# Attention, a gated MLP and a convolved MLP on one core: the first batch's strided heads divided in time, and its first 288 tokens mixed and multiplied on their own

## The chip, the cores and the metric

The kernel runs on one core of one Trainium2 chip. The metric is the device time of one execution in microseconds (us), the median of three runs. The core's engines are TensorE (PE in the profile; its weight loads are PEld), VectorE (DVE), ScalarE (ACT), GpSimd (POOL) and SyncE (SP), which here issues most of the transfers.

## The reference

Four batches of 576 tokens pass through three layers. The second and third work on 512 channels with 1024 hidden ones.

```python
# attention: 8 heads of 64; rel = query - key
mask_local = (rel >= 0) & (rel < 32)                                  # heads 0 to 3
mask_strided = (rel >= 0) & (pos[None, :] % 32 == pos[:, None] % 32)  # heads 4 to 7
attn = softmax(where(mask, q @ k.T / 8, -1e9))
x = attn @ v                                # (4, 576, 512)
# first MLP: each token is mixed with the one before it
xk = mu_k * x + (1 - mu_k) * x_prev
xr = mu_r * x + (1 - mu_r) * x_prev
x = sigmoid(xr @ w_r) * (relu(xk @ w_k) ** 2 @ w_v)
# second MLP, with a convolution over three tokens
h = relu(x @ w_in)
out = (h * sigmoid(conv3(h, conv_w))) @ w_out
```

The weights arrive as 64-bit floats.

## The kernel before

Channels lie on partitions and tokens on columns. A batch of 576 tokens is two chunks of T = 288 tokens, so chunks 0 and 1 are batch 0. Every product of the MLPs is taken with operands divided into a high and a low part (`hi` and `lo`), as three matmuls: high by high, low by high, high by low. `products` issues them for 128 output channels and 288 tokens, per 128 input channels (L789).

**Attention** goes head pair by head pair: p = 0 and 1 are the local heads, p = 2 and 3 the strided ones, two heads in one pair. `load` fetches the pair's queries and keys (tile `qk`) and values (`vt`); `unit(b, p, half, loaded)` computes one half of a pair: scores into PSUM (L594), mask and row maximum on VectorE (L610), exponentials on ScalarE with the row's sum read behind each (L615), one division of the unit on VectorE (L626), transposes on TensorE (L638, L648), a copy to SBUF on either engine (L396/L398 or L657/L659), values on TensorE (L671, L680) and a copy into `xT` (L716 and others). For a local pair a half is a range of tokens: five blocks of 64 queries, then four. For a strided pair it is a range of residues modulo 32: a block holds 3 residues at all 18 of their positions, 54 queries by 54 keys, six blocks in one half and five in the other. So each half of a strided pair has tokens from the whole batch, and no token of the batch is complete before all eight units are. Batch 0's local units have their own form (`wide`: 96 keys, one transpose a block); its strided ones have the form of the other batches.

**Mixing** (`mix`) makes xr or xk for one chunk, or for both chunks of batch 0 at once. For each of four channel tiles it is a scale on ScalarE (L768), a multiply-add on VectorE (L769), a rounding to the high part on ScalarE (L770) and a subtraction for the low part on VectorE (L771).

**Weights** come in pieces of 128 x 512 double words (`fetch`, two buffers `raw`). `narrow` makes 32-bit floats of one (a scale, L411, on ScalarE or VectorE; two shifts and an OR on VectorE, L418, L419, L422), `bring` rounds and subtracts (L461 on ScalarE, L462 on VectorE). w_r is four pieces, w_k and w_v eight each.

**Order.** All work is entered as jobs in a `Plan`, with what they read and write, their cost on each engine that can do them, and their buffers (`bufs`). A list scheduler (`search`, `run`) places the jobs by time and rank when the program is built, over and over with the disturbances whose seeds stand in `STEPS`, and each engine's instructions are issued in the order found. While TensorE would wait, `stir` puts matmuls on idle data into the order (L956). `BEHIND` names the score jobs behind which the first two weight pieces are fetched, `MIXES` the buffers of `mix`. The jobs of batch 0 are entered so: attention of the whole batch; `mix((0, 1), "r", ...)`; each piece of w_r with its products for chunk 0 and chunk 1 (`group_r`, closed by a tanh on ScalarE, L801); `mix((0, 1), "k", ...)`; attention of batch 1; each piece of w_k with its products (a column f, `group_k`) for chunk 0 and chunk 1. Three PSUM banks (`mm`) hold the sums of these products.

Of the kernel before, what the change touches and what calls it, by code (L numbers as in the profile page):

```python
# [15 lines left out]
P = 128  # L16
# [11 lines left out]
WARM, MIXES, BEHIND = 10, 2, (0, 3)  # L28
# [8 lines left out]
STEPS = ((40300000007, 40300000026, 40300000031, 40300000050, 40300000114, 40300000121, 40300000163, 40300000246, 40300000278, 40300000284,  # L37
# [13 lines left out]
HALF_ARRAY = {"sc", "pv"}  # L51
BLOCKS = ("B11", "B21", "B22", "T4", "T1", "T2", "T3")
# [288 lines left out]
def block_kernel(ctx, tc, qkL, qkS, vL, vW, vS, mu_k, mu_r, w_k, w_v, w_r, w_in, conv_w, w_out, ident, mask_l, mask_w, mask_s, out):  # L341
# [13 lines left out]
    ms_sb = const.tile([P, SQ], F32, name="ms_sb")  # L355
# [159 lines left out]

    xT = {}
    unit_before, first_scores, late = [None], [], []

    def load(b, p):

        ns = sum(SB) * SQ
# [200 lines left out]
    def attention(b):  # L722
        xT[b] = space(wx, f"xT{b}", [P, KT, S + 1], tag="xT", bufs=2, parts=9)
        plan.add({"POOL": 0.1}, lambda e: pool.memset(xT[b]()[:, :, 0:1], 0.0), [], [(xT[b], 8)])
        for p in range(4):
            loaded = load(b, p)
            if b == 0 and p == 0:
                consts()
# [563 lines left out]
```

## Time and profile before

| | us |
|---|---|
| median of 3 runs | 509.87 (509.21 to 509.95) |
| the profiled execution | 508.81 |
| its span, first to last instruction | 507.0 |
| TensorE busy in the span | 498.2 |
| VectorE busy | 426.0 |
| ScalarE busy | 390.0 |

The span is a little shorter than the profiled execution's own time, and that one lies below the median of the runs. A busy engine is not an engine at its peak: idle matmuls count as busy too.

### The profile page before, as it was taken

Reading aid. Unit: us, or ns where it says so; the run is one execution under the profiler, and the core shown is the slowest. Engines: PE = TensorE matmul, PEld = TensorE weight load, DVE = VectorE, ACT = ScalarE, POOL = GpSimd, SP = SyncE. Lnnn points to the kernel's source line nnn. Section 1 sums busy time; section 2 is a strip of 40 time slices with the busy share of each in tenths; the row PEclk is TensorE's granted clock in tenths of the full one; section 3 lists DMA queues with packets and bytes.
Section 4 is the critical chain, followed back from the end, with each engine's and each line's share of the span. In section 5 each row is a group of like instructions: output and inputs, shape, how many; then the busy total and the mean of one; then the engine's idle time right before and its main releaser. Section 6 shows DMA issues by size and latency. Waiting matters only on the chain.

```text
span 507.0 us, 13536 instructions
## 1 busy us (share of the span) xinstructions
PE 498.2 (98%) x5114; PEld 480.6 (95%) x5114; DVE 426.0 (84%) x1198; ACT 390.0 (77%) x1137; POOL 1.6 (0%) x15
## 2 busy tenths in 40 slices
PE   8889999999999999999999999999999999999997
PEld 5679999989999999999999999899999999999997
DVE  4999899989757899877899833689999995999993
ACT  5999997999848999758979564487778676767852
POOL 0000000000000000000000000000000000000000
PEclk9999999999999999999999999999999999999999
DMA  8955656994286784676466799938029117200111
GB/s 282 364 185 176 200 187 191 316 307 151 100 268 223 227 277 150 229 247 204 154 200 223 249 309 397 343 110 315 24 64 312 36 22 273 94 35 14 48 48 70
DMA packets 57921, 96.61 MB, mean 191 GB/s; under 512 B 4864, under 2 KB 41984, under 8 KB 57600
## 3 DMA queue, kind: packets, MB, share of 16 engines
q1 hardware_dynamic: 57568, 95.58, 55.4%
q8 instruction: 40, 0.66, 0.6%
q14 instruction: 25, 0.20, 0.1%
q10 hardware_dynamic: 288, 0.16, 0.1%
HBM read 63.95 MB, written 31.78 MB: 189 GB/s over the span
## 4 chain that ended last, share of the span: by engine, by line
PE 88%; ACT 5%; DMA 4%; DVE 2%; issue 1%; SPq 0%; ACTq 0%
PE mm L789 47%; PE hh L1042 17%; PE oz L1139 10%; PE ov L1139 8%; PE sc L594 3%; DMA x_d<-xo 2%; PE pv L680 2%; PE tr L648 1%; DMA raw<-in_w_in 1%; ACT pr L615 1%; DMA qk<-in_qkL 1%; ACT wb L411 1%; ACT mx L768 1%; DVE pr L610 0%; ACT Y L770 0%
## 5 line engine op out<-in xcount | busy, mean ns | idle before, releaser
L789 PE MATMUL mm<-X,wvh 128*128 128x288 f32 x448 | 84.5, 298 | 0.0
L1042 PE MATMUL hh<-x,wi 128*128 128x288 f32 x504 | 75.0, 297 | 1.1 <-ACT b L1050 0.6
L1042 PEld LDWEIGHTS hh<-x,wi 128*128 128x128 f32 x504 | 69.6, 188 | 2.2 <-ACT a L1050 0.9
L789 PE MATMUL mm<-Y,wkh 128*128 128x288 f32 x384 | 68.2, 295 | 0.2 <-ACT rs L801 0.2
L789 PEld LDWEIGHTS mm<-X,wvh 128*128 128x128 f32 x448 | 67.0, 188 | 0.3
L789 PEld LDWEIGHTS mm<-Y,wkh 128*128 128x128 f32 x384 | 56.4, 188 | 0.5 <-ACT rs L801 0.4
L615 ACT ACTIVATE pr<-pr,nmx 128x54 f32<-128x54 f32 (+2 forms) x160 | 53.5, 342 | 4.4 <-DVE nmx L610 4.4
L789 PE MATMUL mm<-Y,wrh 128*128 128x288 f32 x256 | 55.9, 301 | 0.6 <-DVE Y L771 0.3
L1096 DVE SCALAR_TENSOR_TENSOR graw<-hb,cw_sb,graw 128x576 f32<-128x576 f32 x64 | 51.0, 810 | 1.8 <-ACT graw L1091 1.3
L789 PE MATMUL mm<-X,wvl 128*128 128x288 f32 x224 | 47.9, 295 | 0.0
L1115 DVE TENSOR_TENSOR blk<-graw,blk 128x576 fp32r<-128x576 f32 x56 | 40.8, 751 | 6.3 <-ACT blk L1114 6.1
L1114 ACT ACTIVATE blk<-graw 128x576 fp32r<-128x576 f32 x56 | 36.4, 678 | 11.1 <-DVE graw L1120 5.0
L789 PEld LDWEIGHTS mm<-Y,wrh 128*128 128x128 f32 x256 | 42.1, 188 | 1.9 <-DVE Y L771 0.8
L789 PE MATMUL mm<-Y,wkl 128*128 128x288 f32 x192 | 40.8, 294 | 0.0
L789 PE MATMUL mm<-Y,wrl 128*128 128x288 f32 x128 | 38.0, 297 | 0.3 <-DVE wrl L462 0.3
L830 DVE TENSOR_TENSOR X<-sq,X 128x288 fp32r<-128x288 f32 x48 | 21.6, 456 | 19.3 <-ACT X L828 15.0
L789 PEld LDWEIGHTS mm<-X,wvl 128*128 128x128 f32 x224 | 35.9, 188 | 0.0
L615 ACT ACTIVATION_READ_ACCUMULATOR pr<-pr,nmx 128x1 f32 x160 | 31.5, 197 | 0.0
L812 ACT ACTIVATE rl<-mm 128x288 f32<-128x288 f32 x64 | 25.7, 403 | 6.7 <-PE mm L789 6.5
L789 PEld LDWEIGHTS mm<-Y,wkl 128*128 128x128 f32 x192 | 30.7, 188 | 0.0
L1139 PE MATMUL oz<-blk,wo 128*128 128x288 f32 x192 | 30.1, 296 | 0.0
L1097 ACT ACTIVATE graw<-graw 128x576 f32<-128x576 f32 x32 | 21.8, 681 | 9.8 <-DVE graw L1096 9.7
(165 smaller groups left out, 1238.4 us busy)
## 6 DMA issues: line engine op xcount, KB each, us to landing
x_d<-xo SPq DMA_DIRECT2D x42, 288.0 KB, 3.2
x<-x_d SPq DMA_DIRECT2D x21, 576.0 KB, 4.8
wi_d<-ws SPq DMA_DIRECT2D x24, 256.0 KB, 3.7
wo_d<-ws SPq DMA_DIRECT2D x24, 256.0 KB, 2.9
wi<-wi_d SPq DMA_DIRECT2D x6, 896.0 KB, 9.2
qk<-in_qkS SPq DMA_DIRECT2D x8, 599.0 KB, 5.3
out<-ob SPq DMA_DIRECT2D x32, 144.0 KB, 1.7
qk<-in_qkL SPq DMA_DIRECT2D x7, 592.0 KB, 5.1
```

Source lines behind the costliest of these rows:

```text
L594: pe.matmul(bank_of[j]()[to + u:to + u + m, at_[j]:at_[j] + nk], qk()[r, qo[j] + u:qo[j] + u + m], qk()[r, ko[j] + u:ko[j] + u + nk], star ...
L615: act.activation(pr()[:, k], pr()[:, k], AF.Exp, bias=nmx()[:, i:i + 1], scale=-1.0, accum_out=sums()[:, i:i + 1])
L680: pe.matmul(outs_[odd]()[r, i * nq + u:i * nq + u + m], vt()[part, v, r], pt()[part, o:o + m], start=True, stop=True)
L789: pe.matmul(o(), w_cols(name, j, t, part), x_[t](), start=(t == 0 and part == 0 and x_ is xhi), stop=(t == nk - 1 and x_ is xlo))
L812: plan.add({"ACT": 0.295}, lambda e: act.activation(r(), o(), AF.Relu), [o], [r])
L830: plan.add({"DVE": 0.37}, lambda e: dve.tensor_tensor(l_(), sq(), h_().bitcast(F32), ALU.subtract), [sq, h_], [l_])
L1042: pe.matmul(o(), w(hw, j), x()[:, hx, j], start=anew and n == 0 and j == 0, stop=last and n == 2 and j == 1, skip_group_check=True)
L1096: plan.add({"DVE": 0.735}, lambda e, k=k: dve.scalar_tensor_tensor(c(), h()[:, k:k + S], cw_sb[:, k * NF + f:k * NF + f + 1], c(), ALU.mul ...
L1097: plan.add({"ACT": 0.6}, lambda e: act.activation(c(), c(), AF.Sigmoid), [mine], [mine], table="sigmoid")
L1114: plan.add({"ACT": 0.13 + S / 1400}, lambda e, w=w, x=x: act.activation(w()[:, 0], x(), AF.Copy), [mine], [(w, 0)])
L1115: plan.add({"DVE": 0.07 + S / 960}, lambda e, w=w, x=x: dve.tensor_tensor(w()[:, 1], x(), w()[:, 0].bitcast(F32), ALU.subtract), [mine, (w ...
L1139: pe.matmul(o(), w_[s_][1](hw, q), x_()[:, hx, s_], start=anew and m == 0 and i == 0 and s_ == 0, stop=last and m == 1 and i == 2 and s_ = ...
```

## The change

For batch 0 the two halves of a strided pair become halves of time. A block now holds 7 residues at the 9 positions of one half of the tokens: 63 queries. The first half (tokens 0 to 287) sees 63 keys, the second 126, the keys of both halves. Five blocks cover the 32 residues; the last one overlaps the one before it, and only 4 of its residues are stored. These units take the `wide` form: one transpose a block, two copies, values with one PSUM bank. Queries and keys of batch 0 are laid out and loaded for each half on its own (`load_half`), the local ones too.

`attention` can be entered for one half. The jobs of batch 0 are now entered in this order: the first half of all four pairs; mixing r of chunk 0 and its products; mixing k of chunk 0; the second half of all four pairs; mixing r of chunk 1 and its products; mixing k of chunk 1. The four mixings have 288 columns, with three buffers of that size in place of two of 576. There are three `vt` buffers in place of four, the `pr` tile grows from 480 to 630 columns, the second weight piece is fetched behind another score job, and `STEPS` has other seeds for the first of its two plans.

```diff
-WARM, MIXES, BEHIND = 10, 2, (0, 3)
+WARM, MIXES, BEHIND = 10, 3, (0, 2)
...
+CG, CI, CN, VTS = 7, NI // 2, 5, 3
+CQ = CG * CI
...
+    def load_half(p, half):
+
+        qk = space(at, "qk", [P, 2 * sum(SB) * SQ + LQ - SQ], bufs=3, parts=2)
+        vt = space(at, "vt", [P, 6, P], bufs=VTS)
+        row, from_ = P * 4, ((qk0, qk1) if p < 2 else (qkA, qkB))[half]
+        n = from_.shape[-1]
+        if p == 0 and half == 0:
+            cut = 2 * LQ * LEAD + STRIDE
+            dma(lambda: qk()[:, :cut], lambda: from_[p, :, :cut], row * cut, [], [(qk, 0)])
+            dma(lambda: mw_sb, lambda: mask_w, P * 2 * LW * 4, [], [fixed["mw"]], "ACT")
+            dma(lambda: qk()[:, cut:n], lambda: from_[p, :, cut:], row * (n - cut), [], [(qk, 1)])
+            dma(lambda: id_sb, lambda: ident, row * P, [], [fixed["id"]], "ACT")
+        else:
+            dma(lambda: qk()[:, :n], lambda: from_[p % 2], row * n, [], [qk])
+        if p < 2:
+            dma(lambda: vt()[:LW, :LB[half]], lambda: vW[p, :, LB[0] * half:LB[0] * half + LB[half]], LW * 4 * P * LB[half], [], [vt])
+        else:
+            nk = CQ * (1 + half)
+            dma(lambda: vt()[:nk, :CN], lambda: vC[p - 2, :nk], nk * 4 * P * CN, [], [vt])
+        return qk, [vt, vt]
...
-        wide = local and b == 0
-        nb, nq, nk, rows = (LB[half], LQ, LW if wide else LK, P) if local else (SB[half], SQ, SQ, SR)
+        wide = b == 0
+        nb, nq, nk, rows = (LB[half], LQ, LW if wide else LK, P) if local else (CN, CQ, CQ * (1 + half), P) if wide else (SB[half], SQ, SQ, SR)
...
-        pr = space(at, "pr", [P, LB[0] * LW], bufs=3, parts=2)
+        pr = space(at, "pr", [P, 2 * CQ * CN], bufs=3, parts=2)
...
-        if wide:
+        if wide and not local:
+
+            def place(e):
+                d = x()[:, p, 1:].rearrange("p (i r) -> p i r", r=STRIDE)[:, CI * half:CI * half + CI]
+                v = out_()[:, :n].rearrange("p (n i g) -> p n i g", n=nb, i=CI)
+                m = CG * (nb - 1)
+                for d_, v_ in ((d[:, :, :m].rearrange("p i (n g) -> p n i g", g=CG), v[:, :nb - 1]), (d[:, :, m:], v[:, nb - 1, :, CG * nb - STRIDE:])):
+                    if e == "ACT":
+                        act.activation(d_, v_, AF.Copy)
+                    else:
+                        dve.tensor_copy(d_, v_)
+
+            plan.add({"ACT": 0.17 + n / 1400, "DVE": 0.13 + n / 960}, place, outs_, [(x, 2 * p + half)])
+        elif wide:
...
-            y = space(wa, "mx", [P, S], bufs=MIXES)
+            y = space(wa, "mx", [P, T], bufs=MIXES)
...
-    attention(0)
-
-    mix((0, 1), "r", "Y", 0)
+    attention(0, (0,))
+    mix((0,), "r", "Y", 0)
     for m in range(KT):
         bring("wr", m)
-        for c in range(2):
-            group_r(c, m)
-    mix((0, 1), "k", "X", 0)
+        group_r(0, m)
+    mix((0,), "k", "X", 0)
+    attention(0, (1,))
+    mix((1,), "r", "Y", 1)
+    for m in range(KT):
+        group_r(1, m)
+    mix((1,), "k", "X", 1)
     attention(1)
```

## Rows read from the trace of the kernel before

**Rows 1.** Busy time by stretches: us, busy us (x instructions) of each engine, clock, DMA.

```profile
35.44:43.50 8.06, 8.06 (x60) 8.06 (x61) 8.06 (x20) 8.06 (x20) 0.00 (x0) 1.00 0.46 152
43.50:50.20 6.70, 6.70 (x81) 6.45 (x79) 6.68 (x21) 5.50 (x13) 0.00 (x0) 1.00 0.53 169
```

**Rows 2.** TensorE in order of time: start us, us, what, idle before it.

```profile
26.95 0.53 PE L956 MATMUL pv<-idle 128*128 128x288 bf16 x3
...
28.23 0.40 PE L789 MATMUL mm<-Y,wrh 128*128 128x288 f32 x1
...
35.44 0.40 PE L789 MATMUL mm<-Y,wrh 128*128 128x288 f32 x1 [0.28 <-ACT rs L801]
...
43.51 0.43 PE L789 MATMUL mm<-X,wkh 128*128 128x288 f32 x2
...
45.99 0.45 PE L594 MATMUL sc<-qk 64*32 64x64 f32 x32
```

**Rows 3.** ScalarE in order of time, from 47.9 us.

```profile
47.91 0.45 ACT L817 ACTIVATE sq<-rl 128x288 f32<-128x288 f32 x1
48.27 0.41 ACT L812 ACTIVATE rl<-mm 128x288 f32<-128x288 f32 x1
```

**Rows 4.** Groups by form, 10.46 to 50.2 us: busy us, mean ns of one, idle before.

```profile
L615 ACT ACTIVATE pr<-pr,nmx 128x54 f32<-128x54 f32 x22 | 7.2, 341 | 0.0
L422 DVE SCALAR_TENSOR_TENSOR wt<-wb,wt 128x512 int32<-128x512 int32 x8 | 5.4, 687 | 0.0
L610 DVE CUSTOM_DVE_ANT_0 pr<-sc,ms_sb 128x54 f32<-128x54 f32 x22 | 3.3, 199 | 0.0
L615 ACT ACTIVATE pr<-pr,nmx 128x96 f32<-128x96 f32 x9 | 3.2, 363 | 0.0
L615 ACT ACTIVATE pr<-pr,nmx 128x64 f32<-128x64 f32 x5 | 1.7, 344 | 0.0
L610 DVE CUSTOM_DVE_ANT_0 pr<-sc,ml_sb 128x64 f32<-128x64 f32 x9 | 1.5, 216 | 0.0
L610 DVE CUSTOM_DVE_ANT_0 pr<-sc,mw_sb 128x96 f32<-128x96 f32 x6 | 1.3, 254 | 0.2 <-PE sc L594 0.2
L396 ACT ACTIVATE pt<-tr 96x384 f32<-96x384 f32 x2 | 1.0, 484 | 1.1 <-PE tr L638 1.1
L626 DVE TENSOR_TENSOR pr<-pr,rec 128x324 f32<-128x324 f32 x2 | 1.0, 476 | 0.0
L626 DVE TENSOR_TENSOR pr<-pr,rec 128x480 f32<-128x480 f32 x1 | 0.7, 654 | 0.0
L657 ACT ACTIVATE pt<-tr 118x354 f32<-118x354 f32 x1 | 0.5, 487 | 0.0
L396 ACT ACTIVATE pt<-tr 96x256 f32<-96x256 f32 x1 | 0.4, 366 | 0.0
```

**Rows 5.** The same view: the mixing of 576 columns, for r.

```profile
L769 DVE SCALAR_TENSOR_TENSOR mx<-xT,mur_sb,mx 128x576 f32<-128x576 f32 x4 | 3.2, 808 | 0.0
L768 ACT ACTIVATE mx<-xT,mur_sb 128x576 f32<-128x576 f32 x4 | 3.1, 781 | 0.0
L771 DVE TENSOR_TENSOR Y<-mx,Y 128x576 fp32r<-128x576 f32 x4 | 2.9, 747 | 0.0
L770 ACT ACTIVATE Y<-mx 128x576 fp32r<-128x576 f32 x4 | 2.6, 695 | 0.0
```

**Rows 6.** Groups by form, 95 to 180 us: the mixing of 288 columns.

```profile
L771 DVE TENSOR_TENSOR Y<-mx,Y 128x288 fp32r<-128x288 f32 x18 | 8.0, 453 | 0.2 <-ACT Y L770 0.2
L770 ACT ACTIVATE Y<-mx 128x288 fp32r<-128x288 f32 x18 | 7.8, 443 | 0.0
L768 ACT ACTIVATE mx<-xT,mur_sb 128x288 f32<-128x288 f32 x10 | 5.2, 531 | 0.0
L769 DVE SCALAR_TENSOR_TENSOR mx<-xT,mur_sb,mx 128x288 f32<-128x288 f32 x9 | 4.5, 512 | 0.8 <-ACT mx L768 0.7
```

**Rows 7.** Busy time by stretches again, from 5 to 10 us.

```profile
5.00:10.00 5.00, 4.98 (x52) 3.33 (x53) 3.04 (x24) 3.44 (x18) 0.00 (x0) 1.00 1.03 329
```

More of the change, by code (lines that the diff above doesn't have):

```diff
@@ L340, in block_kernel @@
 @with_exitstack
-def block_kernel(ctx, tc, qkL, qkS, vL, vW, vS, mu_k, mu_r, w_k, w_v, w_r, w_in, conv_w, w_out, ident, mask_l, mask_w, mask_s, out):
+def block_kernel(ctx, tc, qk0, qk1, qkA, qkB, qkL, qkS, vL, vW, vC, vS, mu_k, mu_r, w_k, w_v, w_r, w_in, conv_w, w_out, ident, mask_l, mask_w, mask_s, mask_c, out):
     nc = tc.nc
@@ L355, in block_kernel @@
     ms_sb = const.tile([P, SQ], F32, name="ms_sb")
+    mc_sb = const.tile([P, 2 * CQ], F32, name="mc_sb")
     muk_sb = const.tile([P, KT], F32, name="muk_sb")
@@ L557, in unit @@
             mask = fixed["mw" if wide else "ml"]
-            qo = [LQ * j + (S + STRIDE) * (j >= LEAD) for j in range(first, first + nb)]
-            ko = [LQ * LEAD + LQ * (first + j) for j in range(nb)]
+            n1 = LEAD * LQ if not wide else (LEAD, LB[1])[half] * LQ
+            lead = (S if not wide else LB[0] * LQ) + STRIDE
+            at0 = 0 if wide else first
+            qo = [LQ * j + lead * (not (wide and half) and j >= LEAD) for j in range(at0, at0 + nb)]
+            ko = [n1 + LQ * (at0 + j) for j in range(nb)]
+        elif wide:
+            masks, mask = [mc_sb[:, CQ * (1 - half):]] * nb, fixed["mc"]
+            qo, ko = [CQ * j for j in range(nb)], [CQ * nb + 1 + nk * j for j in range(nb)]
         else:
@@ L720, in unit, with attention @@
             plan.add({"ACT": 0.085 * (2 + half) + n / 1400, "DVE": 0.065 * (2 + half) + n / 960}, place, outs_, [(x, 2 * p + half)])
-    def attention(b):
-        xT[b] = space(wx, f"xT{b}", [P, KT, S + 1], tag="xT", bufs=2, parts=9)
-        plan.add({"POOL": 0.1}, lambda e: pool.memset(xT[b]()[:, :, 0:1], 0.0), [], [(xT[b], 8)])
+    def attention(b, halves=range(2)):
+        if b not in xT:
+            xT[b] = space(wx, f"xT{b}", [P, KT, S + 1], tag="xT", bufs=2, parts=9)
+            plan.add({"POOL": 0.1}, lambda e: pool.memset(xT[b]()[:, :, 0:1], 0.0), [], [(xT[b], 8)])
         for p in range(4):
-            loaded = load(b, p)
-            if b == 0 and p == 0:
-                consts()
-            for half in range(2):
+            if b:
+                loaded = load(b, p)
+            for half in halves:
+                if not b:
+                    loaded = load_half(p, half)
+                    if p == half == 0:
+                        consts()
                 unit(b, p, half, loaded)
     def consts():
-        for name, t, x, nb in (("ml", ml_sb, mask_l, P * 2 * LK * 4), ("ms", ms_sb, mask_s, P * SQ * 4), ("muk", muk_sb, mu_k, 2048), ("mur", mur_sb, mu_r, 2048)):
+        for name, t, x, nb in (("ml", ml_sb, mask_l, P * 2 * LK * 4), ("mc", mc_sb, mask_c, P * 2 * CQ * 4), ("ms", ms_sb, mask_s, P * SQ * 4), ("muk", muk_sb, mu_k, 2048), ("mur", mur_sb, mu_r, 2048)):
             late.append(dma(lambda t=t: t, lambda x=x: x, nb, [], [fixed[name]]))
@@ L1226, in _layout @@
     ql, kl = heads_t(q[:, :h]), heads_t(k[:, :h])
-    qkL = np.concatenate([ql[..., :n0], lead, kl, ql[..., n0:]], axis=-1)
+    qkL = np.concatenate([ql[..., :n0], lead, kl, ql[..., n0:]], axis=-1)[1:]
+    m0 = LQ * LB[0]
+    qk0 = np.concatenate([ql[0, ..., :n0], lead[0], kl[0, ..., :m0], ql[0, ..., n0:m0]], axis=-1)
+    qk1 = np.concatenate([ql[0, ..., m0:], kl[0, ..., m0 - STRIDE:]], axis=-1)
+    part = [np.concatenate([(i * STRIDE + r0 + np.arange(CG)) for i in range(NI)]) for r0 in [*range(0, CG * (CN - 1), CG), STRIDE - CG]]
+    lo, hi_, both = [np.concatenate([x[c] for x in part]) for c in (slice(0, CQ), slice(CQ, None), slice(None))]
+    qs, ks = heads_t(q[:, h:])[0], heads_t(k[:, h:])[0]
+    qkA = np.concatenate([qs[..., lo], lead[0, ..., :1], ks[..., lo]], axis=-1)
+    qkB = np.concatenate([qs[..., hi_], lead[0, ..., :1], ks[..., both]], axis=-1)
+    vC = np.ascontiguousarray(v[0, h:][:, both].reshape(2, 2, CN, 2 * CQ, D).transpose(0, 3, 2, 1, 4)).reshape(2, 2 * CQ, CN, 2 * D)
     qkS = np.concatenate([heads_t(q[:, h:, order]), lead[..., :LQ - SQ], heads_t(k[:, h:, order])], axis=-1)
```

40 lines of the change are left out of this document (17 added, 23 removed), and 17 rows, old and new, of the table STEPS.

## The prediction

> **What bounds the kernel now.** I read first the busy time by stretches, then TensorE in order of time over the first 60 us, then the groups by form for what the vector engines do there. TensorE reaches its first useful product of the MLP at 28.23 us; before that it computes only the small matmuls of attention, and idle matmuls fill its holes [rows 2]. Its last wait of any size in the first half of the program ends at 35.44 us; from there it is busy the whole of each stretch, at a granted clock of 1.00 [rows 1, 2]. So a microsecond is won only if TensorE has done more useful work by the time its work becomes continuous, and is then never short again. What feeds it until then is ScalarE and VectorE: from 35.44 to 43.50 us both are busy for 8.06 of 8.06 us, and VectorE for 6.68 of the 6.70 after that [rows 1]. They are the second bound, and the tighter one while the first weight pieces are prepared.
>
> TensorE's side in numbers. A product of 128x288 lands every 0.1325 us when nothing is in its way: from 35.44 to 43.51 us stand 60 of them in 8.07 us [rows 1, 2]. The r products of batch 0 are 2 x 4 x 12 = 96, so 36 of them are done at 35.44. The k products begin at 43.51; two columns f of both halves are 48 products, 6.4 us, and with the scores at 45.99 in between [rows 2] the third column is due at about 50.2 us.
>
> **The change, part by part.** *Moved:* the 48 r products of tokens 0 to 287 (6.4 us) no longer need the second half of attention. They need four units of softmax instead of eight, four mixed tiles of 288 columns and the four pieces of w_r. Tile by tile the second half follows, and the k mixing of the first half can go ahead of that of the second.
>
> *Added on ScalarE and VectorE, attention.* An instruction starts about 0.1 us before the row of the one ahead of it ends: the square at 47.91 is 0.45 long and the next starts at 48.27 [rows 3]. I count an instruction at its duration less 0.1 on ScalarE and less 0.08 on VectorE. For each of the two strided pairs of batch 0, eleven blocks of 54 become five of 63 and five of 126. No row has these widths; they lie between and just beyond the rows of 54 and 96.
> - Exponentials: 11 x 341 ns against 5 x (346 + 379), on the line through 341 and 363: 3.75 to 3.63, -0.1 us [rows 4]. The read of the sum that follows each costs about the 0.1 that overlaps.
> - Masks: 199 and 254 ns; on their line 211 and 293, less overlap: +0.35 us [rows 4].
> - Normalising: 324 and 270 elements become 315 and 630; 1.14 ns an element from 476 and 654 ns gives +0.4 us [rows 4].
> - Transposed weights to SBUF: one copy of 354 columns a unit (487 ns) becomes 384 and 256 (484 and 366): +0.26 a unit, +0.5 us [rows 4].
> - Placing the result: as many elements, two copies in place of two or three: 0.
>
> That is about 1.15 us for each pair, 2.3 us for both.
>
> The Trainium skill ("ScalarE: Activation LUTs", section "What ACT_TABLE_LOAD costs") gives an activation with a bias pointer 280 ns plus 0.833 ns a column, a steeper line than the two rows give; by it, as an estimate, 332 and 385 ns, and the sum would be 0.1 us lower.
>
> *Added, mixing.* Eight tiles of 576 columns become sixteen of 288. From the rows, two of 288 against one of 576, with one overlap less: the scale 2 x 0.43 - 0.68 = 0.18; the multiply-add 2 x 0.43 - 0.73 = 0.13; the rounding 2 x 0.34 - 0.59 = 0.09; the subtraction 2 x 0.37 - 0.67 = 0.07 [rows 5, 6]. 0.47 us a tile, 3.7 us for eight.
>
> So ScalarE and VectorE together get 6.0 us more work, 3.0 each if the copies balance them.
>
> *Added on TensorE.* Ten transposes instead of six a pair, wider scores and values: I estimate 1.4 us a pair, 2.8 in all, from bounds of zero (all in holes) and 2.8 (none). It falls where TensorE waits or computes idle matmuls, as at 26.95 [rows 2], so I take zero. Without that cover it would cost the 2.8.
>
> *Transfers.* Batch 0's loads grow from 11 to 17 (and one more mask), from 4.0 to 4.6 MB by their shapes; but what the first half needs is 2.1 MB. The transfer engines are full from 5 to 10 us, at 329 GB/s [rows 7], so 0.6 MB is 1.8 us of theirs; what lies behind it on SP's queue is w_r's pieces and batch 1's loads. Batch 1's are not wanted until long after, and w_r's now come ahead of the second half's loads. The third unit's data come earlier: 592 + 592 KB stand ahead of it now, about 1.15 MB with masks and v tiles then, 0.1 us of transfer sooner, or 0.6 if the v tiles are put behind; I take 0.3. Three vt and three qk buffers hold a half each, not two halves, so no load waits longer than now. The larger pr tile and the third mx buffer cost no instruction.
>
> **The sum.** What stands against the 6.0 us is slack before the third k column: up to 50.2 us ScalarE has 1.2 us idle [rows 1]; five exponentials and nine masks of batch 1 are done early, 5 x 0.34 + 9 x 0.15 = 3.0 us [rows 4]; and the fourth piece of w_k is almost through, five instructions bounded by 0.6 each [rows 4], which I take at 2.4. Together 6.6 us of the two engines. The extra work just fits: (6.6 - 6.0)/2 = 0.3 us to spare. The k mixing of the second half of tokens, 4 x 1.57 = 6.3 us of the two engines [rows 6], may also wait, which is worth between 0 and 3.1 us; I take 0.2, near nothing, because the second half's products are what TensorE wants next. With that and 0.3 from the earlier data, the two engines allow the whole train of products to come 0.8 us sooner. TensorE's side would allow more (rival A), so the two engines decide: span 507.0 - 0.8 = 506.2. The profiled execution took 508.8, 1.8 us around its span; the median is 509.9, 1.1 above the profiled one. Forecast: 506.2 + 1.8 + 1.1 = 509.1 us. A difference below 0.2%, 1.0 us, is about what a measurement of this kernel can't tell from none; the forecast lies just inside it. Its own range is a gain of 2 to a loss of 0.5 us: 507.9 to 510.4.
>
> **Rivals.**
> A, the products' lead survives. If the two engines have more to put off than I counted, only TensorE's supply decides. At 35.44 us 36 products are done; in the new order all 48 of the first half could be, and 27 of the second (three banks open, nine products each for tiles 0 to 2): 39 more, 5.2 us. If all of the 3.0 us delays the last mixed tile, 2.2 remain. I take 3.0: 506.9. For it: both engines are busy in [rows 1] also with things not due. Against it: the third column.
> B, slower: the two engines lose time early. From 5 to 10 us they are busy 6.5 of 10 us, because few units are in flight [rows 7]. In the new order four chains must run out before the first mixing is complete, and with the slack gone every idle microsecond of both engines is one of the kernel. TensorE's order is fixed at build time, so a product that waits for a late tile also holds the transposes and values of the second half queued behind it, and the copies that wait for those. The same hole once more, 1.8 us each, gives 509.1 + 1.8 = 510.9. It decides as soon as the idle time of the two engines between 10 and 46 us, now nearly nothing, passes about 1.5 us each.
> C, the order does not change: a job's place comes from ranks and times, not from where it is written. If the first product still starts after 27 us, the extra work meets the slack and nothing is won: 509.9 to 511.
> D, the clock. It is 1.00 in every stretch, in which holes are filled [rows 1]. The new order has a hole between the first half's products and the second's. If the clock fell to 1.2 GHz there, the 48 products of the second half would take twice 6.4 us, of which I count half as felt: 512.3. The Trainium skill ("TensorE: Matmul & The Clock Gate", "HAM oscillation — how this bites in real kernels") tells of bursts that each start cold behind a wait; the trace shows no such thing here.
>
> **Chances.** Forecast 0.42 (of it 0.13 faster by over 0.2%, 0.27 within, 0.02 slower); A 0.27, faster; B 0.21 (0.18 slower, 0.03 within); C 0.08 (0.05 within, 0.03 slower); D 0.02. Faster 0.40, same 0.35, slower 0.25. The range must take in A with an error of 0.7 and B with 0.6: 506.2 to 511.5.
>
> **What would show it.** First product of the MLP before 24 us, 48 of them before the second half's last values: the move is right. Exponentials of 63 and 126 columns near 346 and 379 ns, mixing near 0.47 us more a tile: the prices are right. ScalarE and VectorE without idle time from 10 to 50 us, and little of batch 1's softmax before 50 us: the slack was spent as I say. The third k column at about 49.4 us: the sum is right; well before 48, A. The forecast is wrong if TensorE waits on the vector engines between 30 and 50 us (B), or if its work is continuous with no such wait from an earlier time on (A).

## The result, and the profile after

| kernel | median us | range | runs | ratio to before, 95% interval |
|---|---|---|---|---|
| before (in the same comparison) | 509.55 | 508.56 to 509.95 | 6 | |
| changed | 514.66 | 513.33 to 517.19 | 6 | 1.0108 [1.0084, 1.0133] |
| changed, again, in a later comparison | 516.23 | 514.73 to 519.23 | 6 | 1.0140 [1.0112, 1.0169] |

The change makes the kernel 5.1 us slower (7.2 in the later one); 509.1 was forecast, and 514.7 lies above the range of 506.2 to 511.5. The profiled execution of the changed kernel took 515.11 us with a span of 513.3, 6.3 more than before's 507.0.

Busy time by stretches in the changed kernel (answers to [rows 1, 7]; us, busy us of TensorE, its weight loads, VectorE, ScalarE, GpSimd, then clock, DMA share, GB/s):

```profile
5.00:10.00 5.00, 4.25 (x63) 2.62 (x59) 3.56 (x32) 4.09 (x23) 0.00 (x0) 1.00 1.04 298
25.00:30.00 5.00, 4.50 (x67) 3.69 (x68) 3.34 (x17) 3.60 (x12) 0.00 (x0) 1.00 1.09 258
30.00:35.00 5.00, 2.51 (x32) 2.08 (x30) 4.37 (x11) 4.37 (x15) 0.00 (x0) 1.00 0.82 255
35.44:43.50 8.06, 8.06 (x129) 7.29 (x129) 8.06 (x31) 7.92 (x26) 0.00 (x0) 1.00 0.55 164
43.50:50.20 6.70, 6.70 (x53) 6.70 (x52) 6.70 (x22) 6.70 (x18) 0.00 (x0) 1.00 0.79 249
```

TensorE in order of time, changed kernel (answers to [rows 2]):

```profile
21.82 0.40 PE L825 MATMUL mm<-Y,wrh 128*128 128x288 f32 x1
...
29.45 0.30 PE L825 MATMUL mm<-Y,wrh 128*128 128x288 f32 x1
29.59 1.03 PE L995 MATMUL pv<-idle 128*128 128x288 bf16 x7
33.11 0.69 PE L690 MATMUL pv<-pt,vt 96*64 96x64 f32 x16 [2.49 <-ACT pt L398]
...
46.83 0.43 PE L825 MATMUL mm<-X,wkh 128*128 128x288 f32 x2
...
73.47 0.42 PE L825 MATMUL mm<-Y,wvh 128*128 128x288 f32 x2
```

The first r product comes 6.4 us sooner, at 21.82. But the products stop at 29.6 us with 24 of 96 done; idle matmuls fill one microsecond, then TensorE stands for 2.49. At 35.44 us, where the kernel before has 36 r products behind it, this one has 30. The k products begin at 46.83 instead of 43.51, the V products (those with w_v) at 73.47 instead of 69.55. The lead is gone before the second half's attention is through. Both kernels have done their 288 r and k products by the first V product. Of the 3.9 us up to there, TensorE is idle for 1.7 us more (6.1 for 4.4) and busy for 2.2 us more, about 1.0 of that with idle matmuls (55 for 42).

Waits of the changed kernel, 20 to 50 us (us in total, times, longest):

```profile
PE pv L690 <- ACT pt L398: 2.5, 1, 2.5
DVE wt L420 <- DMA raw<-in_w_r: 2.3, 1, 2.3
ACT wb L413 <- DMA raw<-in_w_r: 2.0, 1, 2.0
```

TensorE waits for a copy of ScalarE, and ScalarE and VectorE, just before, for the fourth piece of w_r. It was issued at 21.95 us behind two loads of batch 1 of 592 KB (15.78 and 19.41) and took 8.7 us. The DMA views from 5 to 30 us and of the w_r pieces from 0 to 35 us show the queue, first changed, then before (packets, MB, share of 16 engines; then KB each and median us to landing):

```profile
DMA packets 5013, 7.46 MB, mean 298 GB/s; under 512 B 882, under 2 KB 3410, under 8 KB 5009
...
q1 hardware_dynamic: 5009, 7.41, 104.0%
...
raw<-in_w_r SPq DMA_DIRECT2D x4, 512.0 KB, 7.8
```

```profile
DMA packets 4203, 7.96 MB, mean 318 GB/s; under 512 B 736, under 2 KB 2400, under 8 KB 4198
...
q1 hardware_dynamic: 4198, 7.89, 92.0%
...
raw<-in_w_r SPq DMA_DIRECT2D x4, 512.0 KB, 4.7
```

In these 25 us the transfer engines are busier (104% for 92%) and bring less (7.46 MB for 7.96), in more and smaller packets (1.49 KB for 1.89 on average). In the kernel before they have little left to do from 25 us on; in the changed one they are still full there (1.09):

```profile
25.00:30.00 5.00, 4.30 (x66) 3.23 (x64) 4.99 (x17) 5.00 (x16) 0.00 (x0) 1.00 0.59 192
```

In the whole program the changed kernel reads 64.61 MB for 63.95.

Groups by form, 10.46 to 50.2 us, changed kernel (answers to [rows 4 to 6]; busy us, mean ns of one, idle before):

```profile
L634 ACT ACTIVATE pr<-pr,nmx 128x126 f32<-128x126 f32 x10 | 3.9, 400 | 0.0
...
L634 ACT ACTIVATE pr<-pr,nmx 128x63 f32<-128x63 f32 x8 | 2.6, 332 | 0.0
...
L629 DVE CUSTOM_DVE_ANT_0 pr<-sc,mc_sb 128x126 f32<-128x126 f32 x10 | 2.3, 274 | 0.0
...
L645 DVE TENSOR_TENSOR pr<-pr,rec 128x630 f32<-128x630 f32 x2 | 1.6, 808 | 0.0
...
L645 DVE TENSOR_TENSOR pr<-pr,rec 128x315 f32<-128x315 f32 x2 | 1.0, 482 | 0.0
...
L629 DVE CUSTOM_DVE_ANT_0 pr<-sc,mc_sb 128x63 f32<-128x63 f32 x5 | 0.9, 218 | 0.0
...
L398 ACT ACTIVATE pt<-tr 126x256 f32<-126x256 f32 x2 | 0.8, 406 | 0.0
```

Exponentials of 332 and 400 ns (346 and 379 foreseen), masks of 218 and 274 (211 and 293), normalising of 482 and 808; the r mixing of 288 columns takes 562, 506, 475 and 444 ns where [rows 6] has 531, 512, 443 and 453. On the engines whose rows priced them, the single instructions were right within 40 ns; the widest misses are a copy of 256 columns (406 for 366) and the scale and the rounding of the mixing (31 and 32 ns each). The Trainium skill ("ScalarE: Activation LUTs", "What ACT_TABLE_LOAD costs") gave 332 and 385 ns by its line; the first agrees, the second is 15 ns short of the measured 400, so the two measured points lie on a steeper line than the page's.

### The profile page after: what moved, and what is told of

The parts are those of the page before. It is cut to its first block, busy times and chain, and to the rows that moved or that the text cites. A ratio compares the mean times of both kernels' runs of the same rounds, so it can differ in the third digit from the quotient of the medians.

```text
span 513.3 us, 13583 instructions
## 1 busy us (share of the span) xinstructions
PE 501.3 (98%) x5119; PEld 482.9 (94%) x5119; DVE 430.2 (84%) x1215; ACT 389.2 (76%) x1144; POOL 1.7 (0%) x15
## 3 DMA queue, kind: packets, MB, share of 16 engines
HBM read 64.61 MB, written 31.78 MB: 188 GB/s over the span
## 4 chain that ended last, share of the span: by engine, by line
PE 78%; DMA 9%; ACT 7%; DVE 4%; issue 1%; ACTq 0%; SPq 0%
PE mm L825 39%; PE hh L1081 16%; PE oz L1178 10%; PE ov L1178 8%; DMA x_d<-xo 2%; ACT pr L634 2%; DMA raw<-in_w_r 2%; PE sc L613 1%; DMA raw<-in_w_v 1%; DMA wi_d<-ws 1%; PE pv L699 1%; DMA raw<-in_w_in 1%; ACT mx L804 1%; PE tr L667 1%; PE pv L690 1%
## 5 line engine op out<-in xcount | busy, mean ns | idle before, releaser
L1081 PEld LDWEIGHTS hh<-x,wi 128*128 128x128 f32 x504 | 69.5, 188 | 2.2 <-ACT a L1089 0.9
L825 PE MATMUL mm<-Y,wrh 128*128 128x288 f32 x256 | 57.8, 303 | 0.6 <-ACT rs L837 0.4
L634 ACT ACTIVATE pr<-pr,nmx 128x54 f32<-128x54 f32 (+4 forms) x158 | 53.7, 351 | 3.1 <-DVE nmx L629 3.0
L825 PE MATMUL mm<-X,wvl 128*128 128x288 f32 x224 | 47.9, 295 | 0.0
```

Of the source, the lines that this page charges most:

```text
L634: act.activation(pr()[:, k], pr()[:, k], AF.Exp, bias=nmx()[:, i:i + 1], scale=-1.0, accum_out=sums()[:, i:i + 1])
L825: pe.matmul(o(), w_cols(name, j, t, part), x_[t](), start=(t == 0 and part == 0 and x_ is xhi), stop=(t == nk - 1 and x_ is xlo))
L1081: pe.matmul(o(), w(hw, j), x()[:, hx, j], start=anew and n == 0 and j == 0, stop=last and n == 2 and j == 1, skip_group_check=True)
```

## The experiments

Two theories stood at first. *Late load:* the changed kernel loses what the vector engines wait for a load. *Engine work:* it loses what 6 us of additional ScalarE and VectorE work take. Others came with the runs: TensorE full from 33 us on; the transfers as a whole; the order. Where an expectation speaks of theory 1 and theory 2, it means engine work and TensorE. Times are medians of all runs of a version; each profile is of one execution only.

| version | ratio to before, 95% interval |
|---|---|
| early_wr | 1.0100 [1.0064, 1.0136] |
| late_b1 | 1.0131 [1.0080, 1.0183] |
| aligned | 1.0109 [1.0072, 1.0146] |
| before_more_work | 1.0072 [1.0049, 1.0094] |
| before_mix_halves | 1.0040 [1.0016, 1.0065] |
| before_less_pe | 0.9996 [0.9976, 1.0017] |
| after_less_pe | 1.0086 [1.0056, 1.0115] |
| after_less_mix | 1.0128 [1.0096, 1.0159] |
| mask_early | 1.0145 [1.0121, 1.0169] |
| mask_early_wr | 1.0116 [1.0087, 1.0145] |
| mask_early_wr_less_mix | 1.0080 [1.0061, 1.0098] |
| after_light_loads | 1.0093 [1.0073, 1.0112] |
| before_more_loads | 1.0045 [1.0028, 1.0062] |
| after_replanned | 1.0282 [1.0255, 1.0308] |
| before_replanned | 1.0050 [1.0033, 1.0067] |
| after_replanned_first | 1.0200 [1.0177, 1.0223] |
| before_replanned_first | 0.9981 [0.9965, 0.9997] |

Those whose names begin with "before" are edits of the kernel before, the others of the changed one.

### One load at a time

The fourth w_r piece gets a buffer that is free until later, and is issued right behind the third (early_wr):

```diff
-        raw = space(stg, "raw", [P, WC, 2], I32, bufs=2)
+        raw = space(stg, "raw", [P, WC, 2], I32, bufs=2) if fetched[0] != 3 else <a view of an unused "rs" tile>
+            order: job 125 (fourth w_r piece) right behind job 114 (third)
```

> The changed kernel with every engine's order as it is, but the fourth piece of w_r gets a buffer of its own and is fetched right behind the third, ahead of batch 1's queries and keys. Theory (late piece): both vector engines stand still from 28.2 to 30.6 us because this piece lands at 30.6; with the piece in place the wait of 2.0 and 2.3 us is gone, TensorE's wait of 2.5 us at 30.6 too, and the kernel is 1.8 to 2.6 us faster than the changed kernel (ratio to the kernel before 1.005 to 1.007 in place of 1.011). Rival (engine work alone: the 6 us more work of ScalarE and VectorE sets the time, the wait only uses time that is lost anyway): less than 0.7 us faster, ratio 1.0095 or more.

515.08 us, ratio 1.0100: no gain that can be told. Busy time by stretches:

```profile
10.00:15.00 5.00, 3.07 (x43) 2.16 (x44) 3.58 (x29) 3.47 (x20) 0.00 (x0) 0.76 0.90 292
15.00:20.00 5.00, 4.71 (x80) 3.58 (x78) 3.72 (x18) 3.99 (x16) 0.00 (x0) 0.89 0.97 300
...
25.00:30.00 5.00, 4.26 (x43) 3.08 (x42) 5.00 (x20) 5.00 (x20) 0.00 (x0) 1.00 1.04 227
30.00:35.00 5.00, 4.67 (x82) 3.85 (x81) 5.00 (x18) 5.00 (x16) 0.00 (x0) 1.00 1.05 295
```

The wait at 25 to 35 us is gone: both engines are busy throughout. But time is lost before: from 10 to 20 us VectorE works 7.3 us where the changed kernel's first profile has 9.32, and the clock falls below 1. VectorE waited 2.1 us there for the new mask of the strided heads, which had landed 7.0 us after its issue (4.8 us in the first profile). Whether the move caused that is asked below.

The opposite move holds back batch 1's first two q/k loads until the fourth piece is issued (late_b1), and a third version pads the rows of the strided loads to whole 64 bytes (aligned):

```diff
+            order: jobs 269 and 296 (batch 1's q/k) behind job 185
```
```diff
-    qkA = np.concatenate([..., ks[..., lo]], axis=-1)
+    qkA = np.concatenate([..., ks[..., lo], lead[0, ..., :9]], axis=-1)      # qkB: 14 more
```

> The changed kernel, compute engines in the same order, but batch 1's first two loads of queries and keys (592 KB each) are issued behind the fourth piece of w_r instead of ahead of it. Theory (late piece, because these transfers stand ahead of it): 1.2 MB less ahead of it at about 300 GB/s, so it lands about 4 us sooner, near 26.6 us; no wait of the vector engines for it, 1.0 to 2.5 us faster than the changed kernel (batch 1's scores, which TensorE has in its order at 28 us, may then wait for their own data, which is why it may be less than with the piece early). Rival (the piece is late because its buffer comes free late, at 21.9 us, not because of what is ahead): it lands after 29 us all the same, and less than 0.7 us is won.

> The changed kernel with the rows of the strided queries and keys of batch 0 padded in memory to whole 64 bytes (640 and 960 columns for 631 and 946); the same bytes are moved, in the same order. Theory (the new layout's rows slow the transfers: the engines are full from 20 to 30 us at only 258 to 278 GB/s): the rate rises above 310 GB/s between 10 and 30 us, the fourth piece of w_r lands 1 to 2 us sooner, and the kernel is 0.8 to 2 us faster than the changed one. Rival (the rate is low for another reason): rate, landing and time as in the changed kernel, within 0.7 us.

517.01 us (1.0131) and 515.98 us (1.0109). Padding does nothing, to the time or to the rate (288 GB/s per full share of the engines from 5 to 30 us, 287 in the changed kernel). In late_b1 the fourth piece, issued at 24.26 us, landed 3.5 us later and nothing waited for it: the loads ahead of it, and not its buffer, had made it take 8.7 us. The kernel is no faster for it: TensorE waits 1.5 us for batch 1's q/k, and VectorE is busy only 3.39 of the 5 us from 35 to 40, with batch 1's softmax behind its late loads in the fixed order of the engines: that this load is "not wanted until long after" did not hold for an order that has it early.

To see whether the wait for the mask is of the edits or of the execution, the changed kernel ran again beside versions with the mask issued 1.5 us earlier (mask_early), and with the piece as well (mask_early_wr):

```diff
+            order: job 7 (the mask) behind job 44 (first strided q/k), ahead of the first values
```

> The changed kernel itself, as the one to compare the others of this call with on the same chip. The first run had a ratio of 1.0108 and no wait for the new mask of the strided heads; in four of the five later versions of it VectorE waited about 2 us for that mask near 10 us (it landed 6.5 to 7.9 us after its issue, 4.8 us in the first run), and TensorE's granted clock fell below 0.8 behind it. If that belongs to the chip or the execution and not to the edits, it shows here too and the ratio is 1.011 to 1.015; if it came with the edits, the ratio is 1.010 to 1.011 and the clock 1.0.

> The changed kernel with one load moved: the strided heads' new mask is issued on SyncE ahead of the first values, not behind them (1.5 us earlier). Mask theory (its late landing stops VectorE and lets the clock fall): no wait for it, clock 1.0 near 10 to 20 us, 1 to 3 us faster than the unmoved one of this call wherever that one has the wait. Otherwise: the same time as the unmoved one.

> As the version with the mask moved, and the fourth piece of w_r into its own buffer, issued right behind the third. Late-piece theory (both vector engines stand 2.0 to 2.3 us before 30.6 us for this piece and TensorE 2.5 us at 33 us behind them): about 2 us faster than the version with the mask alone, ratio near 1.007. Engine-work theory (ScalarE and VectorE have the added 6 us to do in any case and are full up to 50 us): under 0.7 us, ratio 1.009 to 1.011.

The unmoved kernel: 1.0140, with the wait for the mask (1.9 us), so it is not of the edits, and early_wr's wait need not have been the price of its move. early_wr's 1.0100 stands between no gain (against 1.0108) and 2 us (against 1.0140); the runs don't settle which. mask_early: 1.0145, no gain. Two of its waits from 5 to 25 us, and two stretches:

```profile
PE sc L613 <- DVE pt L400: 3.2, 1, 3.2
DVE mur_sb L772 <- DMA mur_sb<-in_mu_r: 2.6, 1, 2.6
```
```profile
10.00:15.00 5.00, 1.84 (x27) 1.23 (x25) 1.62 (x14) 2.11 (x13) 0.00 (x0) 0.78 0.92 254
15.00:20.00 5.00, 5.00 (x51) 3.78 (x50) 3.44 (x20) 3.13 (x15) 0.00 (x0) 0.54 0.96 278
```

VectorE now waits 2.6 us for mu_r, 2 KB that stand behind the mask and took 8.0 us; TensorE, behind a copy of VectorE, stands 3.2 us, and its clock is near the lower level (0.54, 1.2 of 2.4 GHz) in the next stretch. mask_early_wr (1.0116) waits for the strided heads' q/k, and for mu_r too:

```profile
PE sc L613 <- DMA qk<-in_qkA: 2.0, 1, 2.0
DVE mur_sb L772 <- DMA mur_sb<-in_mu_r: 1.4, 1, 1.4
```

In each of these profiles another load is the late one. That fits a queue at its limit better than one load in the wrong place, but the profiles are single executions, and early loads vary between executions of one kernel.

### Work of the engines

The kernel before gets the change's work and nothing else: in before_mix_halves the first batch's mixing is issued as two instructions of 288 columns for each of 576; in before_more_work one mask and the copies of each strided unit are also done twice.

```diff
-  act.activation(v(), x()[:, t, 1 + o:1 + o + n_], AF.Copy, scale=mu[:, t:t + 1])
+  for k in range(0, n_, T): act.activation(v()[:, k:k + T], x()[:, t, 1 + o + k:1 + o + k + T], ...)   # all four steps so
-                for i in blocks:                                       # masks
+                for i in [*blocks, *(blocks[:1] if <strided, first section> else [])]:
-                for n, k in ((rows, ...), (nk, ...)):                  # copies of the strided units
+                for n, k in ((rows, ...), (nk, ...)) * (2 if b == 0 else 1):
```

> The kernel before, its order unchanged, with about as much more work of ScalarE and VectorE as the change adds, 6 us of the two together: each mixing instruction of batch 0 issued as two of 288 columns (3.7 us), each copy of transposed weights of its strided units done twice (1.7 us) and one mask of each strided unit done twice (0.5 us); the results are the same. Prediction's slack theory: most of it goes into the slack before the third column, so at most 1 us slower than before (ratio up to 1.002). Rival (engine work alone): in a fixed order both engines are busy without a break from 10 to 46 us, so all of it delays the products, 2 to 3 us slower (ratio 1.004 to 1.006), which would explain half of the loss without any transfer.

> The kernel before, order unchanged, the first batch's mixing issued as two instructions of 288 columns in place of each one of 576: 3.7 us more of ScalarE and VectorE, nothing else. By theory 1 it costs its share of what the 6 us of added work cost in the earlier run (3.7 us for 6.0): about 2.3 us, ratio 1.0045; half its time would be 1.9 us, ratio 1.0036. If the slack that the prediction counted (6.6 us) were there, nothing: ratio 1.000.

3.7 us (0.72%) for some 6 us of work, 2.0 us (0.40%) for the mixing's 3.7. The first is above both expectations, the second as the engine-work theory had it. The prediction's slack would have swallowed both; neither was free.

The profiles of these two versions show more than work, though no load was added. VectorE waits for mu_r, up to 24 us, first before_more_work, then before_mix_halves:

```profile
DVE mur_sb L736 <- DMA mur_sb<-in_mu_r: 1.3, 1, 1.3
```
```profile
DVE mur_sb L736 <- DMA mur_sb<-in_mu_r: 1.0, 1, 1.0
```

In before_more_work the granted clock also falls to the lower level (0.50) ahead of the first r product, which comes at 33.16 us (28.23 in the kernel before):

```profile
25.00:30.00 5.00, 5.00 (x81) 3.14 (x82) 5.00 (x25) 4.97 (x23) 0.00 (x0) 0.50 0.79 283
```

All nine runs of before_more_work have a mean clock of 0.987 to 0.997, while eight of the twelve runs of the kernel before beside them have 0.999 or 1.00. Within the nine, the lower clock does not go with the longer time (516.14 us at 0.997, 512.87 at 0.987), so what the clock costs there stays open. The mixing's 2.0 us do not depend on it: the five runs of before_mix_halves at 1.00 have a median of 512.03 us, the thirteen of the kernel before at 1.00 one of 509.96.

Taking as much out of the changed kernel by mixing for r on 72 columns, first in its plain form, then with mask and piece moved:

```diff
+            cut = 72 if w == "r" and not b else n_      # the four steps of mix() on [:, :cut]; pool.memset(0) on the rest
```

> The changed kernel, order of all engines unchanged; the mixing of the first batch for r (32 instructions of ScalarE and VectorE on 288 columns) is done on 72 columns only and the other columns are filled with zeros by GpSimd, so the output is not the reference's. By the difference between the 576- and the 288-column rows this takes about 6.2 us of ScalarE and VectorE work out, as much as the change added. Theory 1 (these two engines set the first 45 us, so their work counts half): about 3 to 4 us faster than the changed kernel, a ratio of 1.001 to 1.004 to the kernel before. Theory 2 (TensorE is full from 33 us on, with the second half's transposes and values among the products, and sets the time alone): what comes off the engines then only ends the one wait of 2.5 us before 33 us earlier: at most 2.5 us faster, ratio 1.006 to 1.011.

> As the one with mask and piece moved, and the first batch's mixing for r on 72 of 288 columns (the rest filled with zeros by GpSimd, so the output is not the reference's): 6.2 us of ScalarE and VectorE less, as much as the change added. Engine-work theory: with no load late, 2.5 to 3.5 us faster than the one with mask and piece moved, ratio 1.001 to 1.004. TensorE theory (full from 33 us on): 0 to 1.5 us faster.

In the plain form nothing is won (1.0128): the engines wait for w_r (2.1 and 1.7 us) and for the mask (2.3). With mask and piece moved it is 513.08 us against 515.17 (1.0080 against 1.0116, intervals that just overlap, so not clear of noise): about 2.1 us for 6.2 us of work. 4.1 us of loss are left, with ScalarE and VectorE working as much as before, and loads are late again, in the waits of 5 to 45 us:

```profile
PE pv L690 <- DMA vt<-in_vC: 1.4, 1, 1.4
...
DVE wt L420 <- DMA raw<-in_w_k: 1.1, 1, 1.1
```

### TensorE

The 32 products of w_r's low halves with the first batch are left out, 4.3 us of TensorE, in both kernels.

```diff
-                for part, x_ in ((0, xhi), (1, xhi), (0, xlo)):
+                for part, x_ in ((0, xhi), (1, xhi), (0, xlo)) if not <r, first batch> else ((0, xhi), (0, xlo)):
```

> The kernel before, order unchanged, without the same 32 products: 20 of them lie after TensorE's last wait at 35.44 us, 2.7 us. Theory 1: 0 to 1 us faster than the kernel before (ratio 0.998 to 1.0). Theory 2, if TensorE is as full there from 35.44 us on: 2.7 us faster (ratio 0.9947); if the first k product is held by the vector engines: no change.

> The changed kernel, order unchanged; the 32 products of the low halves of w_r with the first batch's tokens are left out (the r gate of the first batch loses its low part). 24 of them lie after 33.1 us, 3.2 us of TensorE by 0.133 us each. Theory 1: 0 to 1 us faster than the changed kernel (ratio 1.009 to 1.011). Theory 2: about 3.2 us faster (ratio 1.0045).

In the kernel before, nothing (0.9996): the k products start at 41.4 us instead of 43.51, but wait 1.6 us for ScalarE and 1.3 for VectorE, and V starts at 69.3. In the changed kernel 1.0086 against 1.0108 and 1.0140 in other comparisons: 1 to 3 us of the 4.3, less than the spread between comparisons allows to settle. Its profile also has a granted clock of 0.84 and 0.82 from 30 to 40 us, where the changed kernel's first profile has 1.00.

### The loads themselves

after_light_loads loads half of each w_r piece; before_more_loads gives the kernel before the change's additional loads, without its work.

```diff
+            pool.memset(whole()[:, 2:], 0); nc.sync.dma_start(out=whole()[:, :2], in_=src[:, :2])      # first four pieces
```
```diff
+  j.emit = <q/k in two column parts>          # local pairs, strided pairs
+  j.emit = <values in two parts>, and nc.sync.dma_start(out=dumped()[...], in_=...) of 378 and 192 columns
```

> The changed kernel, order unchanged; of each of the four pieces of w_r only half is loaded (the other half of the buffer is filled with zeros by GpSimd, so the r gate is not the reference's): 1.05 MB less between 9 and 31 us, which at the 280 GB/s of that stretch is 3.7 us of transfers. Transfer theory (from 5 to 33 us the loads set the pace: whichever comes next is late, mask, mu_r, q/k of the strided heads, w_r in turn): 2 to 3.5 us faster than the changed kernel, ratio 1.004 to 1.008. Engine-work theory: 0 to 0.7 us, ratio 1.010 or more.

> The kernel before, order unchanged, with the change's loads but not its work: the first batch's q/k loads and its strided values are issued in two parts each, and 0.58 MB more is loaded beside them into a buffer that nobody reads. Transfer theory: 0.58 MB at about 300 GB/s is 1.9 us, and most of it shows: 1 to 2.5 us slower, ratio 1.002 to 1.005. Engine-work theory: hidden, ratio 1.000 to 1.001.

The kernel before loses 2.3 us (511.40 against 509.11, 1.0045): what it reads in addition goes into a buffer that nobody reads, and the loads behind it come later. Two of its waits for loads from 5 to 35 us, and two stretches:

```profile
DVE mur_sb L751 <- DMA mur_sb<-in_mu_r: 1.2, 1, 1.2
...
DVE wt L418 <- DMA raw<-in_w_r: 0.8, 1, 0.8
```
```profile
10.00:15.00 5.00, 3.73 (x75) 2.72 (x73) 3.27 (x26) 3.94 (x23) 0.00 (x0) 1.00 0.90 236
...
20.00:25.00 5.00, 4.17 (x78) 2.95 (x76) 5.00 (x28) 4.00 (x21) 0.00 (x0) 0.71 1.05 372
```

The wait for w_r is in no other profile of the kernel before or of its versions. The wait for mu_r is no proof: before_mix_halves and before_more_work have it too, without added loads. Here mu_r landed 5.8 us after its issue (6.8 in the kernel before), but was issued at 7.61 us instead of 5.21, behind SyncE's additional issues. The changed kernel issues it at 4.76. So the 2.3 us are the price of more bytes and more issues together, laid out otherwise than in the changed kernel; no run takes bytes and issues apart. The clock is a third candidate: it was 0.71 and 0.61 from 20 to 30 us, and all twelve runs have a mean clock of 0.993 to 0.999 where the kernel before has 0.999 or 1.00.

after_light_loads, 1.0093, is 0.8 to 2.4 us better than the changed kernel, between the two expectations, and a gain that the spread doesn't settle: it eases the later part of the queue, but the mask's wait (2.1 us) stands ahead of all w_r pieces and stays.

### The order

The first phase is everything up to the last product with w_v, the second phase the second MLP, whose first products write `hh`. Both orders were made for transfers at 350 GB/s. The changed kernel (with the fourth piece in its own buffer) and the kernel before were planned anew in the same way with 280, first the whole program, then the first phase alone.

```diff
-DMA_RATE, DMA_LATENCY = 350.0e3, 3.0
+DMA_RATE, DMA_LATENCY = 280.0e3, 3.0         # *_first: 280 in the first phase, 350 in the second
-STEPS = ((60100000001, ...
+STEPS = ((<new seeds>),
```

> The changed kernel with the fourth w_r piece in its own buffer and a new order of all instructions up to the second phase, planned with a transfer rate of 280 GB/s in place of 350. Order theory (the loss left is the order's, made for transfers that the chip does not reach with these loads): 2 to 4 us faster than the changed kernel, ratio 1.003 to 1.008. Structure theory (more work and more bytes whatever the order): no better than 1 us, ratio 1.009 to 1.013. A ratio under 1 would make it a version to keep.

> The kernel before, planned anew in the same way and with as much search: what the planning alone does. Order theory and structure theory both: 0.998 to 1.004; the difference to the changed kernel planned anew is what the change costs when both have an order made in the same way: about 0.7% or more by the structure theory, under 0.4% by the order theory.

> The new order of the changed kernel (fourth w_r piece in its own buffer, planned with 280 GB/s) up to the second phase; the second phase keeps the order of the kernels before. In the earlier run the first phase's last product ended at 324.0 us, 2.1 us later than in the kernel before and 4.2 us earlier than in the changed one. Structure theory (the change costs work and bytes in any order): ratio 1.004 to 1.007. Order theory: 1.003 or less.

> The kernel before with the new order of its first phase made in the same way, second phase as it was. In the earlier run its first phase ended at 320.7 us, 1.2 us earlier than in the kernel before: ratio about 0.9975, and a version faster than both kernels if it holds. Structure theory: the changed kernel planned anew is 0.5 to 1% slower than this one. Order theory: under 0.4%.

Three of the four came out slower than every expectation: after_replanned (1.0282), after_replanned_first (1.0200) and before_replanned (1.0050). What the profiles still show is the first phase. Its last product ends at 324.0 and 324.4 us in the two changed kernels (328.2 in the changed kernel itself), at 320.7 and 320.8 in the two of before (321.9 in the kernel before). So with orders made alike the first phase of the changed kernel is 3.3 and 3.6 us longer. A late V product is not the loss itself: before_replanned_first begins V at 72.22 us, 2.7 later than the kernel before, and ends the phase 1.1 us sooner, with more of batch 1's attention already done (328 score matmuls before V, 232 in the kernel before). Loads are hardly late in after_replanned_first (0.3 us for the mask, 0.4 for q/k), so late loads are not all of the 3.6 us. From 10 to 15 us its VectorE and ScalarE are still idle for 1.2 and 1.4 us, mostly behind TensorE and each other:

```profile
10.00:15.00 5.00, 4.47 (x80) 3.26 (x79) 3.79 (x29) 3.59 (x15) 0.00 (x0) 1.00 1.08 340
```

But the new order of the changed kernel leaves VectorE's sums for the second phase to the end. Waits of after_replanned_first on TensorE, 50 to 380 us:

```profile
PE hh L1073 <- DVE x L881: 3.4, 4, 1.9
```

The clock is 0.50 in the stretch from 330 to 340 us behind that, and the run is 2% slower than before: the times of these two versions of the changed kernel measure that hand-over between the phases, not the change. An order that saved it might end the first phase later, so the 3.3 and 3.6 us are not the whole price. before_replanned_first is faster than both kernels, 508.63 us against 510.05 (0.9981): small, and not of the change.

## Why the prediction was wrong

*The move, "first product before 24 us": right,* 21.82. "48 of them before the second half's last values" is not what counted: at 35.44 us the changed kernel was 6 products behind, not ahead, and rival A's 39 more were out of sight.

*The prices of single instructions: right,* within 40 ns each. The sum of them was a little low. Masks, with the overlap it states, add 0.41 us a pair and not 0.35; the unit of five blocks had two copies already (382 and 288 ns), so copies add 0.44 and not 0.5. These two cancel. With the measured durations the mixing adds about 4.3 us instead of 3.7, and the whole about 6.9 instead of 6.0, an estimate counted its way; the 0.3 us to spare were not there.

*"The extra work just fits: (6.6 - 6.0)/2 = 0.3 us to spare": wrong, the first step that failed.* The slack was indeed spent (up to 50.2 us no exponential of batch 1, and six pieces narrowed where before eight were), yet the work was felt: 3.7 us when added to the kernel before (2.0 for the mixing alone, at an undisturbed clock), about 2.1, not clear of noise, when taken from the changed one with mask and piece moved. Added to the kernel before, the order stays, so slack that only a new order could use isn't counted there; the second number is from an order that has used it.

*"Transfers: [...] I take 0.3" and "no load waits longer than now": wrong, the second step, by sign.* The 0.6 MB and 1.8 us of transfer time were in the text, and set aside because what lies behind them was thought early enough. More bytes and issues cost 2.3 us in the kernel before, with no work added. That the engines are full at 5 to 10 us the prediction had read [rows 7]; what it had wrong is that the loads behind would still be early enough. In the changed kernel the engines stay full until 30 us and bring less, a w_r piece takes 7.8 us to land (median, 4.7 before), and the fourth stops VectorE for 2.3 us and ScalarE for 2.0. Why they bring less is open (last section).

The two costs, each measured on the kernel before, are 3.7 and 2.3 us, 6.0 together, beside a loss of 5.1 and 7.2. That they simply add was not run, and they are not cleanly apart: the version with more work has late loads and a fallen clock too. So it is shown that neither term was free; how the loss divides between them is not shown. If they add, the earlier products, for which the order was changed, gave nothing visible.

*"TensorE +2.8 [...] I take zero": not refuted for the kernel before* (4.3 us less of its work change nothing), open for the changed one, where 72 r products and the second half's values and transposes lie in one stretch without a hole from 33.11 us. Of the 2.2 us that TensorE is busy longer up to V, some 1.2 are not idle matmuls (an estimate), so zero looks too low there.

*Rival B* had the right side and the right bound: ScalarE and VectorE are idle 2.3 and 3.0 us from 10 to 46 us, past its 1.5. Its price, 1.8 us, was too small. It named few units in flight; in the first profile it is the late w_r piece (2.0 and 2.3 us of that idle time), while the idle time of after_replanned_first from 10 to 15 us is nearer to B's picture. *C* fell, the order did change. *D* fell where it stood: the clock was 1.00 in every stretch shown of the changed kernel's first profile, and four of its six runs have a mean clock of 1.00 and still take 513.3 to 515.1 us. In versions of both kernels the clock does fall, at 10 to 20 us behind late loads, at 20 to 40 us, or at the hand-over to the second phase; there its price stays open.

Left open: from V's first product to the last of the first phase the changed kernel takes 254.7 us (73.47 to 328.2), the one before 252.4 (69.55 to 321.9), for the same products; in the stretch from V's first product to the first of the second phase TensorE is idle 2.73 us (73.5 to 350.5) where before it is 1.35 (69.5 to 344.3). No run took that part alone.

## What to carry to other kernels

When a first stage is divided so that work can start sooner, count bytes and packets ahead of that work before counting instructions: where the transfer engines are at 1.0 already, what is added can make a later load late, and in these runs moving one load left another late. To price such a cost, add it alone to the kernel before, and read from the profile of that run whether anything else moved with it: a later issue, a load that is late without cause, the clock. A late start of the next products is not yet a loss; compare the end of the phase. Slack that two engines show in one order is not slack until the work in it can be put off without a load, a buffer or the next stage's hand-over in its way.

## What was not expected of the hardware

- The transfer engines' rate at full share depends on the loads: 298 GB/s at a share of 1.04 with packets of 1.49 KB on average, 318 at 0.92 with 1.89 KB (per full share 287 and 346). The Trainium skill ("DMA: Bandwidth & Descriptors", "Why small descriptors are slow (HBM only)") gives some three cycles a packet on beats of 32 bytes; as an estimate from that page, 6.0% and 4.8% of overhead, a difference of about 1%. The measured difference is 17%, so that rule alone isn't it. Packet size isn't either: before_more_loads brought 322 GB/s at 0.99 with 1.56 KB, before_more_work 301 at 0.92 with 1.88 KB, both 326 per full share. It goes with the kernel: from 5 to 30 us the profiles of the changed kernel and its versions have 277 to 297 GB/s per full share, those of the kernel before and its versions 326 to 351. The cause is open.
- A load of 2 KB (mu_r) landed 4.7 us after its issue in the first profile of the changed kernel, 8.0 us in mask_early's and 8.9 in before_mix_halves's: with large loads ahead of it, a small one can take as long as they do.
- The same kernel's early loads differ between executions: the mask landed in 4.8 us in the first profile of the changed kernel and in 7.1 in the second, and with it VectorE stood 0 or 1.9 us.
